# Gated attention and SwiGLU on one core: guard rows and second-layer pieces issued earlier, key loads on two queues, weight splits moved behind finished pairs

## The chip, the core and the metric

The kernel runs on one core of a Trainium2 chip. A core has a matrix engine (TensorE, PE in the profile, with its weight loads as PEld), three engines for elementwise work (VectorE or DVE, ScalarE or ACT, GpSimd or POOL) and SyncE (SP), which here only issues transfers. Each engine takes its instructions strictly in the order in which they were written and waits at each for semaphores that others raise. Transfers (DMA) between the chip's memory and the on-chip buffers are issued by an engine and then run on the core's 16 DMA engines. The metric is the device time of one execution in microseconds (us). It is the median of three runs: 1436.97 us, from 1435.83 to 1441.32.

## The reference: what is computed

```python
def _A_ref(x, wqkv, wo):                       # x: 1 x 2048 x 512
    H = 32; Dh = D // H                        # 32 heads of 16
    qkv = (x @ wqkv).reshape(B, S, 3, H, Dh)   # then split into q, k, v
    scores = jnp.einsum("bhqd,bhkd->bhqk", q, k) * Dh ** -0.5
    o = jnp.einsum("bhqk,bhkd->bhqd", softmax(scores), v)
    return o.transpose(0, 2, 1, 3).reshape(B, S, D) @ wo

def _B_ref(x, w1, w3, w2):                     # F = 1792
    return (_silu(x @ w1) * (x @ w3)) @ w2

g = _sigmoid((x * gate_w).sum(-1, keepdims=True))
return g * _A_ref(x, wqkv, wo) + (1 - g) * _B_ref(x, w1, w3, w2)
```

All of it is fp32, and no token is masked.

## The kernel before, in words

**Arithmetic.** [...] Each operand is split into a high half (a cast) and a low half (operand less high half), written hi/lo, xH/xL, wh/wl, and `three` (L94) adds high·high, high·low and low·high into one PSUM bank. So every operand passes a cast and a subtraction first, on POOL for weights and later pieces (L199, L323, L430, L500 and the line behind each), on ACT and DVE for x (L159, L160) and for the first q/k blocks (L186, L187).

**Setup (L334 to L390), written out by hand.** x comes in four blocks of 512 tokens; `transpose_x(b)` transposes block b on PE. `project_qk(0, b, wq)` makes the first 128 columns of q and of k for block b (8 heads) and stores hi and lo of both to memory (`qH_d`, `qL_d`, `kH_d`, `kL_d`), from where `load_q` and `load_k` fetch one head pair into the stacked tiles `Qt` and `Kt`. `project_v(t)` makes V for the 128 tokens of tile t; the sums of tiles 7 to 9 stay in PSUM until L389.

The softmax needs no row maximum as long as a bound on all scores is small. `squares` (ACT, then DVE) sums the squares of each head's weight columns into `rs`, `x_squares` those of each token, and `bound` (L225) multiplies the two largest and sets `flag`. `guard_rows` (L237) writes the bound into rows that go to memory (`m_d`, L247) and back into `Qt` (`load_guard`, L268). `row_maxima` (L277) reads the flag on every engine and branches at L280; the branch's body computes real maxima and is not run with these inputs. The first score (L757) stands behind the branch. `squares` reads six further weight blocks of 256 KB, which SP fetches in two groups of three (L353 and L363, issued at L123) into the three `fr` buffers. `x_gate` (DVE) sums x times gate_w for g.

**The long loop (L777).** A string of letters sets the order: Q is a score product (two matmuls, L757) with its exponential on ACT (L761), P a pair of products with V (L745) that adds up in `acc`, and F one step of `feed`, which gives both halves of PE one matmul each of other work. That other work comes in blocks of 12 or 14 matmuls from `blocks` (L652): the V tiles left, three more chunks of q/k columns, 14 chunks of the hidden layer (L406), then the second layer by token tile (L533, three parts each), then part of the output projection. A half hands its PSUM bank to the other half through a tiny DVE instruction, the tick (L718). Small PSUM banks (`f`) number three.

**Where a block's operands come from.** `load_weights(chunk)` (L312) issues a chunk's two weight fetches on SP into `fr` buffers and puts their split on POOL in the same place. `qk_done` (L424) copies a finished q/k block to a `gs` buffer (DVE, L429; two buffers), splits it on POOL (L430, L431) and stores both halves (SP, L173). `gate_done` and `up_done` form the hidden layer's values and store them to `h_d`. `load_piece(t, q)` (L509) fetches 512 (or 256) hidden rows of token tile t back from `h_d` and splits them on POOL (L500), `load_w2` does the same for the second layer's weights, whose halves take over the tiles of xH and xL. Both stand in the list `loads`, from which one entry is taken at some of the scores.

The transfers of SP and ACT share eight completion semaphores in turn, and a transfer is issued only when the one before it on its semaphore has landed.

Of the kernel before, what the change touches and what calls it, by code (L numbers as in the profile page):

```python
# [17 lines left out]
P = 128  # L18
S = 2048
D = 512  # L20
# [14 lines left out]
def gated_mix_kernel(ctx: ExitStack, tc: tile.TileContext, x, wqkv, wo, w1, w3, w2, gate_w, out):  # L35
# [31 lines left out]
    p1 = ph1.enter_context(tc.tile_pool(name="p1", bufs=1, side="right"))  # L67

# [52 lines left out]
    def load_w(c):  # L121
        w = slot("fr", F32, (P, ND, P))
        nc.sync.dma_start(w, wqkv[:, c:c + P].rearrange("(k p) n -> p k n", p=P))  # L123
        return w
# [50 lines left out]
    def project_qk(c, b, w, between=None):  # L175
        ps = psum2()
        for i in range(2):
            if i and between:
                between()
            for n, (h, xs) in enumerate(((0, xH), (0, xL), (1, xH))):  # L180
                for k in range(ND):
                    nc.tensor.matmul(ps[:, i, :], w[i][h][:, k, :], xs[b][:, k, :], start=n == k == 0,
                                     stop=n == 2 and k == ND - 1)
        hi = p1.tile([P, 2, 512], F32R, name="hi", bufs=2)
        lo = p1.tile([P, 2, 512], F32R, name="lo", bufs=2)
        nc.scalar.activation(hi, ps, AF.Copy)  # L186
        nc.vector.tensor_sub(lo, ps, hi)  # L187
        for i in range(2):
            store_qk(i, c, b, hi[:, i, :], lo[:, i, :])
# [60 lines left out]
    def load_k(j, i, b0=0, b1=NB):  # L250
        c = slice(512 * b0, 512 * b1)
        for h in range(2):
            r = 64 * h
            s = slice(DH * (2 * j + h), DH * (2 * j + h) + DH)
            for o, ks in enumerate((0, 0, 1)):
                nc.sync.dma_start(Kt[i][r + DH * o:r + DH * o + DH, c].bitcast(F32), QD[1][ks][s, c])  # L256
# [20 lines left out]
    def row_maxima():  # L277

        small = nc.values_load(flag, min_val=0, max_val=1)
        with tc.If(small < 1):  # L280
# [4 lines left out]
            for j in range(NPAIR):  # L285
# [14 lines left out]
                mxr = p1.tile([P, 2 * NT], F32, name="mxr")  # L300
# [10 lines left out]

    def load_weights(chunk):  # L312
        out = []
        for n, w in zip("13", chunk["src"]):
            r = slot("fr", F32, (P, ND, P))
            nc.sync.dma_start(r, w.rearrange("(k p) n -> p k n", p=P))
            if chunk["first"]:
                wh = slot("raw", F32R, (P, ND, P))
                wl = slot("raw" if n == "1" else "gw", F32R, (P, ND, P))
            else:  # L320
                wh = slot("fh" + n, F32R, (P, ND, P))
                wl = slot("fl" + n, F32R, (P, ND, P))
            nc.gpsimd.tensor_copy(wh, r)  # L323
            nc.gpsimd.tensor_sub(wl, r, wh)
# [17 lines left out]
    for i in range(2):  # L342
        squares(w0[i], ND * i)
    load_v()
# [8 lines left out]
    ws = [load_w(P * c) for c in range(1, ND)]  # L353
    for t in range(3):
        project_v(t)
# [3 lines left out]
    x_squares(2)  # L359
    project_qk(0, 2, wq)  # L360
    for c in range(1, ND):
        squares(ws[c - 1], c)
    ws = [load_w(D + P * c) for c in range(1, ND)]  # L363
    x_gate(2)
    project_v(4)
    x_squares(3)
    project_v(5)
    transpose_x(3)
    project_v(6)
    for c in range(1, ND):  # L370
        squares(ws[c - 1], ND + c)
    load_q(0, 0, 0)
    load_k(0, 0, 0, 3)
    project_qk(0, 3, wq, bound)
    guard_rows()
    load_guard(0, 0, 0)
    load_k(0, 0, 3, NB)
    x_gate(3)
    load_weights(chunks[0])

# [3 lines left out]
    nc.vector.tensor_scalar(omg, g, -1.0, 1.0, op0=OP.mult, op1=OP.add)  # L384

# [71 lines left out]
    def up_done(f, b):  # L457
        def done(ps):
# [6 lines left out]
            def product():  # L465
# [8 lines left out]
                if f == NF - 1 and b == 0:  # L474
                    loads[0:0] = [lambda q=q: load_piece(0, q) for q in range(2)]
# [7 lines left out]
            if f == NF - 1:  # L483
                loads.extend([lambda c=c: load_w2(c) for c in range(4 * b, min(4 * b + 4, NF))])
                if b == NB - 1:
                    loads.extend([lambda q=q: load_piece(1, q) for q in range(2)])
# [22 lines left out]
    def load_piece(t, q):  # L509
        hi, lo = (slot(SETS[t % 2][2 * q + i]) for i in range(2))  # L510
# [265 lines left out]
    pend, issued, clock = [], 0, 0  # L776
    for i, c in enumerate(order):  # L777
        clock += 1 if c != "P" else 4
        if c == "Q":
# [6 lines left out]
            while soon and order[i + 1] == "P":  # L786
                soon.pop(0)()
            if issued % 128 == (40 if issued // 128 == 5 else 12) and 1 <= issued // 128 < 8:
# [93 lines left out]
```

## Time and profile before

| | |
|---|---|
| median of the runs, and their spread | 1436.97 us (1435.83 to 1441.32) |
| the profiled execution's own time | 1436.01 us |
| its span in the trace | 1434.2 us |
| mean granted PE clock | 0.992 of full |
| PE busy | 1403.3 us |
| ACT busy | 1029.5 us |
| DVE busy | 485.7 us |
| POOL busy | 317.5 us |
| moved by DMA | 141.44 MB |

The span is the profiled execution from its first to its last instruction; 1.8 us of its own time lie around it. A row of an engine's timeline gives the start, the duration, the engine (with a q where its sequencer does it: issuing a transfer, a branch), the line, what is written from what, how many of them, and in brackets how long the engine was idle before and what ended that. A row of waits reads: engine, operation and line, what it waited for, us in total, how many times, the longest. A row of stretches gives for each engine the busy time and the number of instructions, then the granted clock of PE, the DMA engines' mean busy share and the rate. Matmuls overlap, so a matmul's duration is longer than the distance to the next one.

### The profile page before, as it was taken

The numbers are of one execution on the slowest core, as the hardware profiler recorded it, in microseconds if no ns is written. First come the engines' busy times: TensorE is split into PE (matmuls) and PEld (weight loads), VectorE is DVE, ScalarE is ACT, GpSimd is POOL, SyncE is SP. The second block draws the span as 40 slices with busy tenths as digits, with TensorE's granted clock in tenths as the row PEclk, the third lists the DMA queues.
The fourth block names the chain that finished last, engine by engine and source line by source line (L and its number), as shares of the span: only waits on it lengthen the run. The fifth ranks groups of instructions, "written<-read, shape, count | busy, mean of one in ns | idle before, by whom it ended". The sixth has DMA issues, their size and how long they took to land.

```text
span 1434.2 us, 29035 instructions
## 1 busy us (share of the span) xinstructions
PE 1403.3 (98%) x11471; PEld 835.6 (58%) x11471; DVE 485.7 (34%) x1079; ACT 1029.5 (72%) x1147; POOL 317.5 (22%) x356
## 2 busy tenths in 40 slices
PE   9879989999999999999999999989999999999998
PEld 7656555656565565655656566545655555555556
DVE  5511111154555555455555545531111110011113
ACT  4447666777777777777777777766778787788870
POOL 5011433211101110011011021552423222233240
PEclk9989999999999999999999999999999999999999
DMA  7722444543213433223232522543534443355344
GB/s 200 176 54 53 130 113 129 135 112 75 57 44 87 108 68 83 62 67 91 53 83 70 119 77 60 133 119 79 131 92 97 99 102 78 76 128 116 88 131 174
DMA packets 112863, 141.44 MB, mean 99 GB/s; under 512 B 16496, under 2 KB 70768, under 8 KB 109744
## 3 DMA queue, kind: packets, MB, share of 16 engines
q1 hardware_dynamic: 110576, 135.72, 38.4%
q10 hardware_dynamic: 2144, 3.80, 0.7%
q8 instruction: 92, 1.51, 0.5%
q14 instruction: 51, 0.42, 0.1%
HBM read 90.70 MB, written 48.76 MB: 97 GB/s over the span
## 4 chain that ended last, share of the span: by engine, by line
PE 92%; DMA 1%; POOL 1%; SPq 0%; issue 0%; ACT 0%; DVE 0%; POOLq 0%; DVEq 0%; ACTq 0%
PE acc L745 32%; PE f L406 26%; PE S L757 19%; PE f L533 11%; PE f L415 1%; PE f L619 1%; DMA fr<-in_A_wqkv_dram 0%; PE f L96 0%; PE f L97 0%; PE f L98 0%; PE S L98 0%; PE S L97 0%; PE S L96 0%; DMA sg<-h_d 0%; SPq L256 0%
## 5 line engine op out<-in xcount | busy, mean ns | idle before, releaser
L761 ACT ACTIVATE p<-S 128x1024 f32<-128x1024 f32 x1024 | 967.3, 1024 | 338.6 <-PE S L757 338.2
L745 PE MATMUL acc<-p,V 128*17 128x512 f32 x4096 | 473.7, 596 | 0.0
L757 PE MATMUL S<-Qt,Kt 50*128 50x512 f32 x2048 | 410.8, 412 | 12.5 <-SPq L280 12.2
L757 PEld LDWEIGHTS S<-Qt,Kt 50*128 50x128 f32 x2048 | 186.9, 185 | 185.1 <-issue 76.5
L745 PEld LDWEIGHTS acc<-p,V 128*17 128x17 f32 x4096 | 103.6, 97 | 278.8 <-issue 278.5
L449 DVE RECIPROCAL sg<-sg 128x64 f32<-128x64 f32 x448 | 209.6, 517 | 53.0 <-issue 50.9
L406 PE MATMUL f<-xH,fh 64*128 64x512 f32 x1024 | 205.9, 391 | 4.8 <-DVE tick L718 4.8
L406 PE MATMUL f<-xL,fh 64*128 64x512 f32 x1024 | 206.0, 392 | 0.0
L406 PE MATMUL f<-xH,fl 64*128 64x512 f32 x1024 | 205.5, 391 | 0.0
L323 POOL CAST fh<-fr 128x512 fp32r<-128x512 f32 x32 | 20.4, 637 | 443.8 <-DMA fr<-in_B_w_dram 423.4
L406 PEld LDWEIGHTS f<-xH,fh 64*128 64x128 f32 x1024 | 99.6, 187 | 26.8 <-DVE tick L718 5.2
L718 DVE MEMSET tick<- 1x1 f32 x196 | 11.6, 59 | 302.3 <-PE f L533 165.1
L406 PEld LDWEIGHTS f<-xL,fh 64*128 64x128 f32 x1024 | 100.1, 187 | 20.8
L406 PEld LDWEIGHTS f<-xH,fl 64*128 64x128 f32 x1024 | 99.1, 185 | 20.1
L533 PE MATMUL f<-xH,fh 64*128 64x512 f32 x224 | 64.9, 395 | 5.6 <-POOL fh L500 5.6
L533 PE MATMUL f<-xH,fl 64*128 64x512 f32 x224 | 66.3, 395 | 0.0
L533 PE MATMUL f<-xL,fh 64*128 64x512 f32 x224 | 65.8, 394 | 0.0
L441 DVE COPY gs<-f 128x512 f32<-128x512 f32 x56 | 38.7, 692 | 60.4 <-PE f L406 59.0
L533 PE MATMUL f<-xH,raw 64*128 64x512 f32 x192 | 56.2, 391 | 0.0
L726 DVE COPY u<-acc 128x512 f32<-128x512 f32 x32 | 22.1, 692 | 96.7 <-PE acc L745 96.7
L447 DVE TENSOR_SCALAR sg<-sg 128x512 f32<-128x512 f32 x56 | 25.3, 451 | 81.4 <-ACT sg L446 81.4
L552 DVE SCALAR_TENSOR_TENSOR y<-f,omg,y 128x512 f32<-128x512 f32 x32 | 24.0, 751 | 77.4 <-PE f L533 77.4
(224 smaller groups left out, 1350.7 us busy)
## 6 DMA issues: line engine op xcount, KB each, us to landing
Kt<-kH_d SPq DMA_DIRECT2D x124, 128.0 KB
h_d<-sg SPq DMA_DIRECT2D x56, 256.0 KB
sg<-h_d SPq DMA_DIRECT2D x43, 256.0 KB
fr<-in_B_w_dram SPq DMA_DIRECT2D x42, 256.0 KB
Qt<-qH_d SPq DMA_DIRECT2D x128, 64.0 KB
Kt<-kL_d SPq DMA_DIRECT2D x62, 128.0 KB
fr<-in_A_wqkv_dram SPq DMA_DIRECT2D x18, 256.0 KB
Qt<-qL_d SPq DMA_DIRECT2D x64, 64.0 KB
```

Of the source, the lines that this page charges most:

```text
L323: nc.gpsimd.tensor_copy(wh, r)
L406: return nc.tensor.matmul(ps, w[i == 2][r, k, :], (xL if i == 1 else xH)[b][r, k, :], start=n == 0 and not second, stop=n == 3 * ND - 1 an ...
L415: return nc.tensor.matmul(ps, (xL if i == 2 else xH)[b][r, k, o:o + P], wv[k][i == 1][r, :], start=n == 0 and not second, stop=n == 3 * ND ...
L441: nc.vector.tensor_copy(gs, ps)
L447: small.append(lambda: nc.vector.tensor_scalar(sg, sg, 1.0, None, op0=OP.add))
L449: small.append(lambda q=q: nc.vector.reciprocal(sg[:, q:q + 64], sg[:, q:q + 64]))
L533: ins = nc.tensor.matmul(ps, hs[t][q][i == 2][r, P * o:P * o + P], (w2L if i == 1 else w2H)[q][r, o, :], start=n == 0 and not second, stop ...
L552: nc.vector.scalar_tensor_tensor(y, ps, omg[:, t:t + 1], y, op0=OP.mult, op1=OP.add)
L726: nc.vector.tensor_copy(u, acc)
L745: nc.tensor.matmul(acc[r:r + DH + 1, :], V[:, k, 2 * j + h, :], p[:, h, :], start=k == 0, stop=k == NT - 1)
L757: nc.tensor.matmul(ps[:, h, :], Kt[i][r:r + 50, P * k:P * k + P], Qt[i][r:r + 50, t:t + 512], start=True, stop=True)
L761: nc.scalar.activation(p, ps, AF.Exp, scale=SCALE)
```

## The change

The edits, in the order of the program:

1. The six weight blocks for `squares` are fetched right behind the squares of the first two, issued by ACT, into six tiles of their own (pool `sqp`). The `squares` calls themselves stand between `project_v(0)`, `(1)` and `(2)`.
2. `x_squares(3)` follows `x_squares(2)`. `bound`, block 3's transpose and `guard_rows` stand ahead of `project_qk(0, 3)`; so do the first head pair's loads (all but the key loads of block 3), the loads of the guard rows, the two gate sums left, g and chunk 0's weight fetch. `project_v(6)` follows the block.
3. `project_qk` stores K before Q. The six key loads of block 3 are issued by SP for one head and by ACT for the other.
4. The split of a chunk's weights (all but the first chunk's) is put on POOL six scores after its fetch is issued.
5. The first two pieces of token tile 1 are fetched with those of tile 0, when the hidden layer's block 0 is done, into tiles (`wo2`, `wo3`) that the output weights take later. Before, they stood last in `loads`.
6. A tile in the branch that isn't run gets eight more columns.

```diff
-    def load_w(c):
-        w = slot("fr", F32, (P, ND, P))
-        nc.sync.dma_start(w, wqkv[:, c:c + P].rearrange("(k p) n -> p k n", p=P))
+    def load_w(c, tile=None, e=nc.sync):
+        w = tile if tile is not None else slot("fr", F32, (P, ND, P))
+        e.dma_start(w, wqkv[:, c:c + P].rearrange("(k p) n -> p k n", p=P))
         return w
...
-        for i in range(2):
+        for i in (1, 0):
             store_qk(i, c, b, hi[:, i, :], lo[:, i, :])
...
-    def load_k(j, i, b0=0, b1=NB):
+    def load_k(j, i, b0=0, b1=NB, e=(nc.sync, nc.sync)):
...
-                nc.sync.dma_start(Kt[i][r + DH * o:r + DH * o + DH, c].bitcast(F32), QD[1][ks][s, c])
+                e[h].dma_start(Kt[i][r + DH * o:r + DH * o + DH, c].bitcast(F32), QD[1][ks][s, c])
...
+    splits, issued = [], 0
+
+    def split(hi, lo, src):
+        nc.gpsimd.tensor_copy(hi, src)
+        nc.gpsimd.tensor_sub(lo, src, hi)
+
     def load_weights(chunk):
...
             if chunk["first"]:
...
+                split(wh, wl, r)
             else:
...
-            nc.gpsimd.tensor_copy(wh, r)
-            nc.gpsimd.tensor_sub(wl, r, wh)
+                splits.append((issued + 6, lambda a=(wh, wl, r): split(*a)))
...
     for i in range(2):
         squares(w0[i], ND * i)
+    ws = [(ND * i + c, load_w(i * D + P * c, sqp.tile([P, ND, P], F32, name=f"s{i}{c}"), nc.scalar))
+          for i in range(2) for c in range(1, ND)]
     load_v()
     project_qk(0, 0, wq, lambda: transpose_x(1))
...
     load_x(3)
-    ws = [load_w(P * c) for c in range(1, ND)]
-    for t in range(3):
-        project_v(t)
+    project_v(0)
+    for n, w in ws[:ND - 1]:
+        squares(w, n)
+    project_v(1)
+    for n, w in ws[ND - 1:]:
+        squares(w, n)
+    project_v(2)
     transpose_x(2)
     fill_k()
     project_v(3)
     x_squares(2)
+    x_squares(3)
     project_qk(0, 2, wq)
-    for c in range(1, ND):
-        squares(ws[c - 1], c)
-    ws = [load_w(D + P * c) for c in range(1, ND)]
+    project_v(4)
+    bound()
+    transpose_x(3)
+    guard_rows()
     x_gate(2)
-    project_v(4)
-    x_squares(3)
     project_v(5)
-    transpose_x(3)
-    project_v(6)
-    for c in range(1, ND):
-        squares(ws[c - 1], ND + c)
     load_q(0, 0, 0)
     load_k(0, 0, 0, 3)
-    project_qk(0, 3, wq, bound)
-    guard_rows()
     load_guard(0, 0, 0)
-    load_k(0, 0, 3, NB)
     x_gate(3)
-    load_weights(chunks[0])
-
...
+    load_weights(chunks[0])
+    project_qk(0, 3, wq)
+    load_k(0, 0, 3, NB, (nc.sync, nc.scalar))
+    project_v(6)
...
                 if f == NF - 1 and b == 0:
-                    loads[0:0] = [lambda q=q: load_piece(0, q) for q in range(2)]
+                    loads[0:0] = [lambda t=t, q=q: load_piece(t, q) for t in range(2) for q in range(2)]
...
                 if b == NB - 1:
-                    loads.extend([lambda q=q: load_piece(1, q) for q in range(2)])
                     hurry = True
...
     def load_piece(t, q):
-        hi, lo = (slot(SETS[t % 2][2 * q + i]) for i in range(2))
+        if t == 1 and q < 2:
+            both = wk.tile([P, 2, 512], F32R, name=f"wo{2 + q}")
+            hi, lo = both[:, 0, :], both[:, 1, :]
+        else:
+            hi, lo = (slot(SETS[t % 2][2 * q + i])[:] for i in range(2))
...
+            while splits and splits[0][0] <= issued:
+                splits.pop(0)[1]()
```

Where this moves instructions is shown for three engines. First ACT near the program's start; `raw<-fr` at L222 (L223 after) are the squares of the first two weight blocks, `xH1` is the high half of x block 1, `hi` that of the first q/k block. Before:

```order
L222 ACTIVATE raw_193<-fr_114 128x512
L222 ACTIVATE raw_196<-fr_116 128x512
L159 ACTIVATE xH1_236<-f_238 128x512
L159 ACTIVATE xH1_236<-f_239 128x512
L159 ACTIVATE xH1_236<-S_240 128x1024
L186 ACTIVATE hi_275<-S_223 128x1024
```

And after:

```order
L223 ACTIVATE raw_199<-fr_119 128x512
L124 DMA s01_202<-in_A_wqkv_dram 128x4x128
L124 DMA s02_204<-in_A_wqkv_dram 128x4x128
L124 DMA s03_206<-in_A_wqkv_dram 128x4x128
L124 DMA s11_208<-in_A_wqkv_dram 128x4x128
L124 DMA s12_210<-in_A_wqkv_dram 128x4x128
L124 DMA s13_212<-in_A_wqkv_dram 128x4x128
L160 ACTIVATE xH1_251<-f_253 128x512
L160 ACTIVATE xH1_251<-f_254 128x512
L160 ACTIVATE xH1_251<-S_255 128x1024
```

Six issues now stand between the squares and the copies of x block 1. The fifth (`s12`) uses the semaphore of the first V weight's fetch, the sixth (`s13`) that of the second's.

Next SP between the last q/k block's stores and the branch (L280, L281 after). Before:

```order
L173 DMA kL_d_84<-lo_655 128x512
L247 DMA m_d_85<-sg_665 32x4x512
L247 DMA m_d_85<-sg_666 32x4x512
L268 DMA Qt0_105<-m_d_85 2x1024 x2
L256 DMA Kt0_107<-kH_d_83 16x512 x2
L256 DMA Kt0_107<-kL_d_84 16x512
L256 DMA Kt0_107<-kH_d_83 16x512 x2
L256 DMA Kt0_107<-kL_d_84 16x512
L316 DMA fr_687<-in_A_wqkv_dram 128x4x128
L316 DMA fr_693<-in_A_wqkv_dram 128x4x128
L279 TENSOR_LOAD flag_129
```

And after:

```order
L269 DMA Qt0_108<-m_d_88 2x1024 x2
L323 DMA fr_641<-in_A_wqkv_dram 128x4x128
L323 DMA fr_647<-in_A_wqkv_dram 128x4x128
L174 DMA kH_d_86<-hi_678 128x512
L174 DMA kL_d_87<-lo_679 128x512
L174 DMA qH_d_84<-hi_678 128x512
L174 DMA qL_d_85<-lo_679 128x512
L257 DMA Kt0_110<-kH_d_86 16x512 x2
L257 DMA Kt0_110<-kL_d_87 16x512
L280 TENSOR_LOAD flag_132
```

The guard rows' way through memory and the weight fetches moved ahead of the last stores, and three of the six key loads went to ACT, where they stand behind `hi` of the last block and ahead of V tile 6's copy.

Last POOL, where the long loop's first weight chunk but one is split; `sg<-gs` and `gs<-gs,sg` split a finished q/k block, `fh1`, `fl1`, `fh3`, `fl3` are halves of weights. Before:

```order
L431 TENSOR_TENSOR gs_6324<-gs_6324,sg_6325 128x512
L323 CAST fh1_6334<-fr_6332 128x512
L324 TENSOR_TENSOR fl1_6335<-fr_6332,fh1_6334 128x512
L323 CAST fh3_6340<-fr_6338 128x512
L324 TENSOR_TENSOR fl3_6341<-fr_6338,fh3_6340 128x512
L430 CAST sg_6363<-gs_6362 128x512
L431 TENSOR_TENSOR gs_6362<-gs_6362,sg_6363 128x512
```

And after:

```order
L439 TENSOR_TENSOR gs_6328<-gs_6328,sg_6329 128x512
L438 CAST sg_6363<-gs_6362 128x512
L439 TENSOR_TENSOR gs_6362<-gs_6362,sg_6363 128x512
L316 CAST fh1_6338<-fr_6336 128x512
L317 TENSOR_TENSOR fl1_6339<-fr_6336,fh1_6338 128x512
L316 CAST fh3_6342<-fr_6340 128x512
L317 TENSOR_TENSOR fl3_6343<-fr_6340,fh3_6342 128x512
```

One finished pair went ahead of the split. The same happens at the next chunk's split; at the others POOL's order is as before. In the fetches of pieces, SP's two for token tile 1 moved from behind all second-layer weights to the place of tile 0's first two: three piece fetches, then the twelve loads of the next head pair and its guard rows, then the fourth.

## What the change should do to the time

> **What bounds the kernel now.** I read the busy times first, then what TensorE (PE) waits for, then stretches of two microseconds around each wait for the granted clock, then the instructions around each wait.
>
> ```profile
> PE 1403.3 (98%) x11471; PEld 835.6 (58%) x11471; DVE 485.7 (34%) x1079; ACT 1029.5 (72%) x1147; POOL 317.5 (22%) x356
> PE S L757 <- SPq L280: 12.2, 1, 12.2
> PE f L533 <- POOL fh L500: 5.6, 1, 5.6
> PE f L406 <- DVE tick L718: 4.8, 1, 4.8
> PE f L230 <- DVE am L227: 1.6, 1, 1.6
> PE f L97 <- POOL fl L200: 0.7, 1, 0.7
> ```
>
> PE is busy 98% of the span, and the change leaves all its 11,471 matmuls in place. So the time can only move through PE's waits. Three are long: A (12.2 us, before the first score), B (4.8, a q/k product), C (5.6, the first product of token tile 1). Each is a single wait. The stretches below (columns: PE, PEld, DVE, ACT, POOL busy; granted clock; DMA share; GB/s) show what else they cost.
>
> ```profile
> 72.00:74.00 2.00, 0.00 (x0) 0.00 (x0) 1.13 (x2) 0.00 (x0) 0.00 (x0) 0.87 0.18 36
> 86.00:88.00 2.00, 2.00 (x16) 1.95 (x13) 0.06 (x1) 1.32 (x2) 0.00 (x0) 0.71 1.23 229
> 198.00:200.00 2.00, 0.18 (x2) 0.18 (x4) 0.69 (x2) 0.00 (x0) 0.62 (x2) 0.95 0.79 285
> 202.00:204.00 2.00, 2.00 (x16) 0.39 (x12) 0.00 (x0) 1.02 (x1) 0.00 (x0) 0.70 0.36 132
> 960.00:962.00 2.00, 0.00 (x0) 0.00 (x0) 0.00 (x0) 0.00 (x0) 1.92 (x3) 0.74 0.75 239
> 966.00:968.00 2.00, 2.00 (x12) 0.34 (x8) 0.00 (x0) 0.95 (x1) 1.84 (x4) 0.55 0.00 0
> ```
>
> With half and full clock as the two states, a mean of 0.87 over 2 us puts the drop at 73.5, 4.5 us after PE stopped (81.17 - 12.2 = 69.0). In the same way the drop is at 199.8 in B (4.8 after the stop at 195.0) and at 961.0 in C (4.2 after 956.8). Full clock returns at 87.2, 203.2 and 967.8. From PE's restart (81.17, 199.82, 962.40) that is 6.0, 3.4 and 5.4 us at half clock, and half of it is lost: 3.0, 1.7 and 2.7 us. So A costs 15.2, B 6.5 and C 8.3 us, 30 in all.
>
> **Wait A: the order of the last q/k block.** Columns: start, duration, engine, line, instruction; SPq is SyncE issuing.
>
> ```profile
> 49.44 0.48 PE L96 MATMUL f<-fh,xH 128*128 128x512 f32 x1
> 52.32 1.11 PE L182 MATMUL S<-xH,wh 128*128 128x512 f32 x4
> 60.20 1.02 ACT L186 ACTIVATE hi<-S 128x1024 fp32r<-128x1024 f32 x1 [4.18 <-PE S L182]
> 63.39 0.44 SPq L173 DMA_DIRECT2D kL_d<-lo  x1
> 63.93 1.01 SPq L247 DMA_DIRECT2D m_d<-sg  x2
> 68.76 0.96 SPq L268 DMA_DIRECT2D Qt<-m_d  x2
> 72.99 0.42 SPq L256 DMA_DIRECT2D Kt<-kL_d  x1
> 73.45 0.97 SPq L316 DMA_DIRECT2D fr<-in_A_wqkv_dram  x2
> 81.17 1.42 PE L757 MATMUL S<-Qt,Kt 50*128 50x512 f32 x4 [12.21 <-SPq L280]
> 60.00:66.00 6.00, 6.00 (x28) 4.82 (x28) 4.49 (x11) 1.02 (x1) 0.00 (x0) 1.00 0.60 169
> ```
>
> SP stands from 64.94 to 68.76 behind the landing of the guard rows, and then issues the two guard loads, six key loads and two weight fetches before it reaches the branch. From its last issue (74.42) to PE's restart pass 6.75 us of flag load, branch and event releases. Nothing in the change touches those, so I keep 6.75.
>
> After the change the guard rows, their loads and the weight fetches stand ahead of the last block's stores, so only kH, kL, qH, qL and three key loads (the other three are ACT's) precede the branch. PE reaches the last block earlier by the 1.6 us wait for the bound and by V tile 6, now behind it: 2.9 us (49.44 to 52.32). The bound and guard rows now take two of the three small PSUM banks ahead of V tile 5; a new wait there, between 0 and 1.6 (the bound's own), is taken at 1.0, since the bound must still come through DVE. Moving the squares adds the early wait of the next part, +3.5. So the copy to hi starts at 60.2 - 1.6 - 2.9 + 1.0 + 3.5 = 60.2, where it was, and the kL store goes out at 63.4 less the places of the two q stores that no longer precede it (0.9): 62.5. Its landing is bounded by the kL store at wait B (below: 196.58 to 199.08 at latest, 2.5) and the guard rows (63.93 to 68.76: 4.8); I take 4.5, near the upper one, since the weight fetches now share the queues. Then three key loads at 0.44 (1.3), then 6.75: PE restarts at 75.1, I say 75.5 for the gate sums that ACT's copy to hi now has ahead of it. PE runs out at 69.0 - 1.6 + 1.0 + 3.5 = 71.9 and idles 3.6 us, shorter than any of the three delays (4.2, 4.5, 4.8) after which the clock fell. So A gives 81.2 - 75.5 = 5.7, and the 3.0 of half clock: 8.7.
>
> ACT's three key issues stand ahead of V tile 6's copy, and V tile 9 needs that bank: PE is waiting for the keys then anyway. Storing K before Q delays only qH and qL, whose last block the first scores don't read. The early weights of chunk 0 need no cover: their split ran on an idle POOL. The eight more columns of mxr lie in the branch that isn't taken.
>
> **The price of the moved squares.** Six weight loads move from SP (30 and 47 us) to ACT, ahead of ACT's copies of x block 1.
>
> ```profile
> 8.94 1.16 ACT L222 ACTIVATE raw<-fr 128x512 f32<-128x512 f32 x2
> 13.62 1.09 ACT L159 ACTIVATE xH<-f 128x512 fp32r<-128x512 f32 x2 [3.52 <-PE f L156]
> 16.94 1.20 PE L182 MATMUL S<-xH,wh 128*128 128x512 f32 x4 [0.22 <-DVE xL L160]
> 17.00 0.61 POOL L199 CAST fh<-fr 128x512 fp32r<-128x512 f32 x1 [2.62 <-DMA fr<-in_A_wqkv_dram]
> L123 SPq DMA_DIRECT2D fr<-in_A_wqkv_dram x8: 397/504/5077, 2.6 to 47.7; - x8
> ```
>
> ACT is free at 10.1 and needed at 13.62; six issues at the median 0.50 would take 3.0 and fit. But the transfers of SP and ACT share eight completion semaphores, and each waits for the one before it on its own. The sixth of ACT's follows the second V weight, which lands just ahead of its cast at 17.00. So ACT would issue it then and begin x block 1's copies at about 17.8 instead of 13.62: 4.2 us late, and so are the subtraction and the second block's product (21.1 instead of 16.94). The later 0.7 us wait for a V weight is absorbed: +3.5. Bounds: 0 (the weight lands in time) and 5.3 (V's fetch shares the queues with four of the six). PE is idle for 4.4 us here, a little more than the earliest drop (4.2, C), so I charge B's loss of 1.7. The +3.5 is already in the 75.5.
>
> [...]
>
> **Wait B: the split ahead of a finished pair.**
>
> ```profile
> 185.35 0.69 DVE L429 COPY gs<-f 128x512 f32<-128x512 f32 x1 [1.84 <-issue]
> 190.74 0.61 POOL L323 CAST fh<-fr 128x512 fp32r<-128x512 f32 x1 [12.30 <-DMA fr<-in_A_wqkv_dram]
> 194.59 0.62 POOL L430 CAST sg<-gs 128x512 fp32r<-128x512 f32 x1
> 196.58 0.34 SPq L173 DMA_DIRECT2D kL_d<-gs  x1
> 199.08 0.69 DVE L429 COPY gs<-f 128x512 f32<-128x512 f32 x1 [7.20 <-DMA kL_d<-gs]
> 199.82 0.80 PE L406 MATMUL f<-xH,fh 64*128 64x512 f32 x2 [4.77 <-DVE tick L718]
> ```
>
> A q/k result is copied at 186.0, but POOL stands at the split of weights that land at 190.7 and turns to the pair at 194.59. Its gs buffer comes free only when its store has landed; the DVE copy at 199.08 waited for that, the tick behind it too, and PE for the tick. With the pair ahead of the split, POOL takes it at 186.1 (two operations, 2.0), and its stores land near 191, four microseconds before the copy that PE waits behind. Next late is the following pair, still behind the split: its buffer comes free near 199, its reader wants it near 200, so I charge nothing and keep up to 1 us. B gives 4.8 + 1.7 = 6.5. The other split that moves shows no wait of PE before.
>
> **Wait C: token tile 1's first piece.**
>
> ```profile
> 897.41 1.34 POOL L501 TENSOR_TENSOR xL<-fr,xH 128x512 fp32r<-128x512 f32 x1
> 895.89 0.64 SPq L263 DMA_DIRECT2D Qt<-qH_d  x1
> 902.89 0.57 SPq L268 DMA_DIRECT2D Qt<-m_d  x2
> 957.35 1.05 SPq L499 DMA_DIRECT2D fr<-h_d  x2
> 961.74 0.61 POOL L500 CAST fh<-fr 128x512 fp32r<-128x512 f32 x1
> 962.40 0.79 PE L533 MATMUL f<-xH,fh 64*128 64x512 f32 x1 [5.63 <-POOL fh L500]
> 965.56 0.61 POOL L500 CAST fr<-sg 128x512 fp32r<-128x512 f32 x1
> ```
>
> The piece is fetched at 957.35, behind everything else, and POOL casts it at 961.74. After the change both pieces are split near 905. PE goes on at 956.8; the next piece (965.56 now) moves up by the two splits no longer ahead of it, 3.8 us, to 961.7 plus 1.9 of its own, and PE wants it about four blocks' work later, near 966. That leaves two microseconds, so I charge nothing: C gives 5.6 + 2.7 = 8.3. The price lies near 896: three of four piece fetches go ahead of SP's twelve loads of the next head pair, and the third needs a buffer that POOL frees at 898.75. The loads then end near 907 instead of 903.5. They are issued 26 scores ahead of use, 34 us at 1.32 us each ((1434.2 - 81.2)/1024), so 26 us of cover hide 4.
>
> **Sum.** Against the profiled execution's own 1436.0 (span 1434.2): -8.7 + 1.7 - 6.5 - 8.3 = -21.8, so 1414.2. The median of the runs is 1.0 above that execution: I predict 1415.
>
> **Rivals.** R1: ACT isn't held up, the sixth load finds its semaphore free. Then PE restarts at 72.0 and the 1.7 goes: 5.2 less, 1410. For it: ACT's 3.52 us of idle time ahead of 13.62 hold six issues; against it: the cast at 17.00 that waited 2.62 for its landing.
>
> R2: the last keys land late. The queues were 0.60 full in 60 to 66 and get 0.5 MB of weights ahead of the last stores, 3 us at the 169 GB/s of that row. With 3 us more twice over (store and load), PE restarts at 81 and the clock falls again: A gives nothing, 8.7 back, 1424. [...]
>
> R3, no change to be measured: the waits of B and C pass to the next pair and the next piece, whose margins are 1 and 2 us; both come back in full (14.8): 1430.
>
> R4, slower: at 896 SP is stuck behind the piece fetches, because their buffers come free only with POOL, and POOL waits for PE's last reading of the x tiles that the second-layer weights take. The loads of the next head pair come late and scores stop. It costs nothing up to 26 us, each further one in full; past 55 us (26 + 21.8 + 7) the kernel is slower by over 0.5%. Against it: POOL frees the buffer at 898.75 in the row above. A stall of 60 us would give 1449.
>
> **Chances.** Forecast (1411 to 1420) 0.58, R1 0.12, R2 0.13, R3 0.07, R4 0.10. Of R4 I leave part to mechanisms like it that I don't see. The range takes forecast, R1 and R2, 0.83, widened by the bounds of the landing (2 us down) and of the early wait: 1408 to 1427. Faster by over 0.5% (7 us, about what a measurement of this kernel can tell from no change): 0.83; R3 goes to no change, 0.07; R4 to slower, 0.10.
>
> **What would show it.** PE's wait for the branch shrinks to some 3.6 us with the clock at 1.00 after it, restart near 75.5; a new wait of about 4 us at the second block's product near 17 to 21, with ACT's copies of x block 1 behind its last weight issue; no wait of a q/k product for the tick near 195; PE's first product of tile 1 without a wait near 935, and its piece split near 890 (905 less what A and B give). I am wrong if ACT's issues don't wait, if the last keys land after 70, or if any of PE's waits outside these places exceeds 2 us.

## The result and the profile after

The median fell from 1436.40 to 1417.47 us (four runs each, the three of the table above among them; 1435.52 to 1441.32 before, 1417.2 to 1417.8 after). The ratio is 0.9861, 95% interval 0.9839 to 0.9884: the changed kernel is 18.9 us faster, 1.2 to 1.6%. The forecast was 1415, with 1408 to 1427 around it.

The profiled execution of the changed kernel has a span of 1415.7 us, 18.5 less than before (1434.2). Its busy times and the waits of PE (waited for, us in total, times, longest):

```profile
PE 1400.2 (99%) x11471; PEld 833.0 (59%) x11471; DVE 487.0 (34%) x1079; ACT 1028.9 (73%) x1147; POOL 319.5 (23%) x356
PE S L183 <- DVE xL L161: 4.5, 1, 4.5
PE f L97 <- ACT V L212: 3.1, 1, 3.1
PE f L97 <- DVE xL L161: 0.9, 1, 0.9
PE S L768 <- PEq L281: 0.6, 1, 0.6
```

The waits for the split (B, 4.8 us) and for tile 1's piece (C, 5.6) are gone, and so is the one for the bound. The 12.2 us wait ahead of the first score has become 3.1 plus 0.6. The first row is new: it is the early wait behind ACT's weight fetches.

Where the time went is best read from the same instruction in both traces, here the exponential of some of the 1024 scores (start in us, columns before, after, difference):

```
score     before    after    difference
   16      105.5    101.2     -4.33
   80      189.6    185.1     -4.43
   88      206.6    195.7    -10.96
  656      951.8    941.8    -10.00
  664      970.9    952.3    -18.63
 1016     1392.2   1373.7    -18.55
```

So the setup gives 4.4 us, wait B 6.5 and wait C 8.6. Between scores 88 and 656 the kernel after loses 1.0 again, in many small steps, while PE is busy throughout.

**Wait A after.** Rows of ACT, SP and PE around the last q/k block, the events behind the branch (how many, shortest, median and longest in ns, first and last start in us), and three stretches (columns as in the prediction):

```profile
62.32 1.01 ACT L187 ACTIVATE hi<-S 128x1024 fp32r<-128x1024 f32 x1
63.95 0.96 SPq L323 DMA_DIRECT2D fr<-in_A_wqkv_dram  x2
65.55 0.97 SPq L174 DMA_DIRECT2D kL_d<-lo  x1
72.27 0.30 SPq L257 DMA_DIRECT2D Kt<-kL_d  x1
72.68 0.60 ACT L212 ACTIVATE V<-f 128x512 f32<-128x512 f32 x1 [9.35 <-DMA kL_d<-lo]
73.33 0.79 PE L97 MATMUL f<-fh,xH 128*128 128x512 f32 x1 [3.15 <-ACT V L212]
79.44 0.93 PE L768 MATMUL S<-Qt,Kt 50*128 50x512 f32 x4 [0.62 <-PEq L281]
L281 SPq EVENT_SEMAPHORE  x8: 17/17/17, 77.6 to 78.2; - x8
L281 PEldq EVENT_SEMAPHORE  x1: 51/51/51, 78.9 to 78.9; - x1
64.00:68.00 4.00, 4.00 (x19) 3.23 (x18) 0.68 (x2) 0.00 (x0) 0.00 (x0) 1.00 1.02 178
72.00:74.00 2.00, 0.67 (x2) 0.57 (x3) 0.00 (x0) 0.60 (x1) 0.20 (x1) 0.67 0.96 104
78.00:80.00 2.00, 1.38 (x6) 0.65 (x7) 0.69 (x1) 0.00 (x0) 0.00 (x0) 0.63 0.17 45
```

SP no longer stands behind the guard rows. But the last kL store, issued at 65.55, lands only at 72.2, 6.7 us later, in a queue that is full (share 1.02). The first score comes at 79.44, 1.7 earlier than before and 3.9 later than the prediction's 75.5, of which 1.7 are the early half clock that it charged apart. PE doesn't stand idle all that time: V tile 9 runs at 73.33, late, because V tile 6's copy stands on ACT behind the key loads, and at half clock (72.7 to 79.5), so that it ends only at 78.8. So PE is the last to pass the branch (78.9; SP is through at 78.2), and the V tile holds the first score by some 0.9 us, an estimate from these two rows and from 0.25 us between SP's event and the first score where SP is the last (79.26 and 79.51 in the kernel with V tile 6 ahead of the keys). The half clock is over when the scores begin.

**The early wait, B and C after**, in rows of ACT, PE, DVE, POOL and SP:

```profile
10.26 7.14 ACTq L124 DMA_DIRECT2D s<-in_A_wqkv_dram  x4
17.45 1.09 ACT L160 ACTIVATE xH<-f 128x512 fp32r<-128x512 f32 x2 [7.87 <-DMA fr<-in_A_wqkv_dram]
20.76 1.51 PE L183 MATMUL S<-xH,wh 128*128 128x512 f32 x4 [4.55 <-DVE xL L161]
180.92 0.69 DVE L437 COPY gs<-f 128x512 f32<-128x512 f32 x1 [1.84 <-issue]
181.67 0.61 POOL L438 CAST sg<-gs 128x512 fp32r<-128x512 f32 x1 [7.65 <-DVE gs L437]
183.66 0.34 SPq L174 DMA_DIRECT2D kL_d<-gs  x1
186.26 0.61 POOL L316 CAST fh<-fr 128x512 fp32r<-128x512 f32 x1 [2.62 <-DMA fr<-in_A_wqkv_dram]
189.65 0.69 DVE L437 COPY gs<-f 128x512 f32<-128x512 f32 x1 [2.20 <-DMA kL_d<-gs]
190.43 0.06 DVE L729 MEMSET tick<- 1x1 f32 x1
883.14 4.70 SPq L506 DMA_DIRECT2D fr<-h_d  x3
892.27 0.60 POOL L507 CAST wo<-fr 128x512 fp32r<-128x512 f32 x1
893.52 0.58 SPq L269 DMA_DIRECT2D Qt<-m_d  x2
```

The four last issues of ACT take 7.14 us. The last of them starts at 17.02, right behind the landing of the second V weight, and the copies of x block 1 stand behind it. In B POOL takes the finished pair at once and splits the weights behind it. In C the piece is split at 892, and SP's loads of the next head pair end at 894.1.

### The profile page after: what moved, and what is told of

It is laid out like the page before. It is cut to its first block, busy times and chain, and to the rows that moved or that the text cites. A ratio compares the mean times of both kernels' runs of the same rounds, so it can differ in the third digit from the quotient of the medians.

```text
span 1415.7 us, 29018 instructions
## 1 busy us (share of the span) xinstructions
PE 1400.2 (99%) x11471; PEld 833.0 (59%) x11471; DVE 487.0 (34%) x1079; ACT 1028.9 (73%) x1147; POOL 319.5 (23%) x356
## 4 chain that ended last, share of the span: by engine, by line
PE 94%; ACT 0%; DVE 0%; issue 0%; ACTq 0%
PE acc L756 33%; PE f L414 27%; PE S L768 19%; PE f L544 11%; PE f L630 1%; PE f L423 1%; PE f L97 0%; PE f L98 0%; PE f L99 0%; PE S L99 0%; PE S L98 0%; PE S L97 0%; ACT p L772 0%; PE acc L99 0%; PE acc L98 0%; PE acc L97 0%
## 5 line engine op out<-in xcount | busy, mean ns | idle before, releaser
L414 PE MATMUL f<-xL,fh 64*128 64x512 f32 x1024 | 206.0, 391 | 0.0
L414 PE MATMUL f<-xH,fh 64*128 64x512 f32 x1024 | 205.9, 390 | 0.0
L414 PE MATMUL f<-xH,fl 64*128 64x512 f32 x1024 | 205.5, 390 | 0.0
L414 PEld LDWEIGHTS f<-xH,fh 64*128 64x128 f32 x1024 | 99.7, 186 | 21.8 <-DVE tick L729 0.4
L544 PE MATMUL f<-xH,fl 64*128 64x512 f32 x208 | 61.8, 390 | 0.0
L544 PE MATMUL f<-xL,fh 64*128 64x512 f32 x208 | 60.9, 391 | 0.0
L544 PE MATMUL f<-xH,fh 64*128 64x512 f32 x208 | 59.8, 391 | 0.0
L563 DVE SCALAR_TENSOR_TENSOR y<-f,omg,y 128x512 f32<-128x512 f32 x32 | 24.0, 751 | 78.2 <-PE f L544 78.2
```

What stands on the lines that cost most here:

```text
L414: return nc.tensor.matmul(ps, w[i == 2][r, k, :], (xL if i == 1 else xH)[b][r, k, :], start=n == 0 and not second, stop=n == 3 * ND - 1 an ...
L544: ins = nc.tensor.matmul(ps, hs[t][q][i == 2][r, P * o:P * o + P], (w2L if i == 1 else w2H)[q][r, o, :], start=n == 0 and not second, stop ...
L563: nc.vector.scalar_tensor_tensor(y, ps, omg[:, t:t + 1], y, op0=OP.mult, op1=OP.add)
```

## The experiments

Ratios are to the kernel before on the same chip, whose medians there were 1438.4 to 1439.4. Its runs spread over 5 us, those of the changed kernel over 1.6 in both comparisons together. To have a measure for the kernels that are set against the changed one, that was run once more beside them, with no edit:

> The changed kernel itself once more, beside the kernel before, as the measure for the experiments, whose runs of the kernel before had medians of 1438.4 to 1439.1 where the first comparison had 1436.4. Theory (the time of the changed kernel is the same in these runs, and only the kernel before scatters with where its half-clock phases fall): 1417 to 1418.5. Rival (these runs are slower by 2 us for any kernel): 1419 to 1420, and the differences of the experiments from the changed kernel shrink or grow by 2 us.

1417.86 us (1417.55 to 1418.79), ratio 0.9852 (0.9834 to 0.9870). The changed kernel's median holds to 0.4 us, so differences from 1417.5 below can be read to about half a microsecond where the runs of a kernel lie close together. Starts in a trace are less certain: the first score of this run's profiled execution is at 81.05, 1.6 later than in the first one. About half of that is there when the early wait ends (21.5 against 20.8), and about half comes from the half clock behind it, which lasted 6.8 us (19.7 to 26.5) where it had lasted 3.4.

**Each of the three parts alone.** First only the split behind the pair, on the kernel before:

```diff
-            nc.gpsimd.tensor_copy(wh, r)
-            nc.gpsimd.tensor_sub(wl, r, wh)
+                splits.append((issued + 6, lambda a=(wh, wl, r): split(*a)))
...
+            while splits and splits[0][0] <= issued:
+                splits.pop(0)[1]()
```

> The kernel before with one edit: a weight chunk's split is put on POOL six scores after its fetch. Theory (wait B is one local wait and costs its idle time and the half clock behind it): PE's 4.8 us wait for the tick goes, the clock stays at 1.00 near 200 us, the median is 6.5 us lower, 1429.9 against 1436.4. Rival (the wait passes to the next pair): a wait of 2 to 5 us at a later q/k product, gain under 3 us.

1429.35 us, ratio 0.9934 (0.9915 to 0.9954), that is 6.6 to 12.2 us lower. PE's wait for the tick is gone, and no later product takes its place. The rival is out; the forecast 6.5 lies just below the interval.

Then only the two pieces early:

```diff
-                    loads[0:0] = [lambda q=q: load_piece(0, q) for q in range(2)]
+                    loads[0:0] = [lambda t=t, q=q: load_piece(t, q) for t in range(2) for q in range(2)]
...
-                    loads.extend([lambda q=q: load_piece(1, q) for q in range(2)])
...
+        if t == 1 and q < 2:
+            both = wk.tile([P, 2, 512], F32R, name=f"wo{2 + q}")
+            hi, lo = both[:, 0, :], both[:, 1, :]
```

> The kernel before with one edit: the first two pieces of token tile 1 fetched early into tiles of their own. Theory: PE's 5.6 us wait near 957 goes with its half clock, 8.6 us lower, 1427.8. Rival (the next piece is late instead): a wait of 2 us or more at tile 1's third piece, gain 3 to 5 us.

1429.19 us, ratio 0.9935 (0.9918 to 0.9952): 6.9 to 11.8 lower, as the theory had it, and no wait at the third piece.

Then only the setup:

```diff
-                splits.append((issued + 6, lambda a=(wh, wl, r): split(*a)))
+                split(wh, wl, r)
...
-                    loads[0:0] = [lambda t=t, q=q: load_piece(t, q) for t in range(2) for q in range(2)]
+                    loads[0:0] = [lambda q=q: load_piece(0, q) for q in range(2)]
...
+                    loads.extend([lambda q=q: load_piece(1, q) for q in range(2)])
```

> The changed kernel without the other two edits (weights split at once, tile 1's pieces last in the list). Theory (the three parts add): 4.4 us lower than before, 1432.0, with the early wait of 4.5 us near 17 to 21 and PE's first score near 79.4. Rival (the parts act on each other): a difference from -4.4 of more than 2 us.

1434.77 us, ratio 0.9974 (0.9964 to 0.9984): 2.3 to 5.2 lower. The early wait (4.5) and the V tile's (3.3) are there as in the changed kernel. The three gains sum to 22.0, against 18.9 and 21.6 for the whole change in its two comparisons: the parts add, within their intervals.

**The early wait.** On the changed kernel, the fifth and sixth fetch of ACT moved behind the second block's copy:

```diff
+    ws = load_ws([(0, 1), (0, 2), (0, 3), (1, 1)])
...
     project_qk(0, 1, wq)
+    ws += load_ws([(1, 2), (1, 3)])
```

> The changed kernel with the fifth and sixth weight fetch of ACT issued behind the second q/k block's copy instead of ahead of x block 1's copies. Theory (ACT's wait for the second V weight makes the early stall, and the stall passes on to the first score through the last q/k block): the 4.5 us wait and its half clock go, the last block's hi copy starts near 57 and the first score near 74, 5.5 us lower than the changed kernel, 1412.0. Rival (the first score is set by the transfers of the last keys, whose queue is full from 64 to 72): the early wait goes but the first score comes no earlier than 77.5, at most 2 us lower, 1415.5.

1421.41 us, with runs from 1417.61 to 1424.15: 3.9 higher than the changed kernel by the medians, a miss of both. Its waits of PE, and the squares on ACT, in an execution of 1423.73 us:

```profile
PE f L97 <- ACT V L212: 10.2, 2, 7.3
PE S L183 <- DVE xL L161: 0.2, 1, 0.2
23.60 1.14 ACTq L124 DMA_DIRECT2D s<-in_A_wqkv_dram  x2
37.09 0.63 ACT L223 ACTIVATE raw<-s 128x512 f32<-128x512 f32 x1 [6.00 <-DMA s<-in_A_wqkv_dram]
40.75 0.63 ACT L223 ACTIVATE raw<-s 128x512 f32<-128x512 f32 x1 [3.03 <-DMA s<-in_A_wqkv_dram]
68.92 1.01 ACT L187 ACTIVATE hi<-S 128x1024 fp32r<-128x1024 f32 x1
84.96 1.18 PE L772 MATMUL S<-Qt,Kt 50*128 50x512 f32 x4 [2.17 <-PEq L281]
```

The early wait is gone (0.2). But the two blocks, fetched at 23.6 behind block 2 of x, land at 37 and 40.7. The copies of V stand on ACT behind their squares, and PE waits 7.3 us for a bank. The theory's second half shows all the same: the last block's copy is 6.6 later than in the changed kernel, and the first score 5.5.

So the squares of these two were moved too, behind the third q/k block's copy:

```diff
-    for n, w in ws[ND - 1:]:
-        squares(w, n)
+    squares(ws[ND - 1][1], ws[ND - 1][0])
     project_v(2)
...
     project_qk(0, 2, wq)
+    for n, w in ws[ND:]:
+        squares(w, n)
     project_v(4)
```

> As the kernel with the fifth and sixth weight fetch behind the second block's copy, but the squares of these two stand behind the third q/k block's copy, so that no copy of V waits for them. Theory (the early stall passes on to the first score): no wait over 1 us ahead of the first score but the V tile's, the last block's hi copy near 56 to 57, the first score near 73.5 to 74.5, 5 to 6 us lower than the changed kernel. Rival (the transfers are the bound: with PE's setup 6 us shorter the queue is full for all of it): the last keys land more than 8 us after their store, first score at 77 or later, at most 2.5 us lower.

1414.76 us, 2.7 lower than the changed kernel. The first score came at 77.83, 1.6 earlier, not 5 to 6. That is the rival's first score, and about its time, but for another reason: the last kL store took 6.8 us to land, no longer than in the changed kernel, while PE now waited 2.3 for the bound, whose squares came late, and 0.8 for a V weight.

Then only the sixth fetch was moved, the one that waits for the second V weight, and to a place ahead of block 2 of x:

```diff
+    ws = load_ws([(0, 1), (0, 2), (0, 3), (1, 1), (1, 2)])
     load_v()
     project_qk(0, 0, wq, lambda: transpose_x(1))
+    ws += load_ws([(1, 3)])
```

> The changed kernel with one fetch moved: the sixth weight block for the squares is issued behind the first q/k block's copy, ahead of block 2 of x in the queues; the first five stay. Theory (that one issue makes the early stall, and the first score follows the last block's hi copy at a fixed distance of about 17 us): no wait near 17 to 21, no half clock there, the last block's hi copy at 56.5 to 58, first score at 73.5 to 75, 1411.5 to 1413.5. Rival (something else holds the last block, the gate sums on DVE or the queues): hi no earlier than 60, first score no earlier than 77, 1415 or more.

1413.13 us (1412.91 to 1413.97), 4.3 lower than the changed kernel; 0.9822 of the kernel before (0.9802 to 0.9841). Its rows around the copies of x block 1, the last block and the first score:

```profile
14.35 1.09 ACT L160 ACTIVATE xH<-f 128x512 fp32r<-128x512 f32 x2 [3.53 <-PE f L157]
17.67 1.20 PE L183 MATMUL S<-xH,wh 128*128 128x512 f32 x4 [0.23 <-DVE xL L161]
59.31 1.01 ACT L187 ACTIVATE hi<-S 128x1024 fp32r<-128x1024 f32 x1
62.55 1.04 SPq L174 DMA_DIRECT2D kL_d<-lo  x1
69.29 0.30 SPq L257 DMA_DIRECT2D Kt<-kL_d  x1
75.37 0.93 PE L772 MATMUL S<-Qt,Kt 50*128 50x512 f32 x4 [0.71 <-SPq L281]
```

The copies wait for PE again, not for a landing; the early wait and its half clock are gone. The time is as forecast. The first score is 4.1 earlier: 3.0 by the last block's copy, and 1.1 behind SP's last issue, because V tile 9 is here through the branch with SP (74.8 and 75.0) and no longer behind it. That one issue made the early wait, and the wait passes on to the end. The last block's copy moved less than forecast (59.31, not 56.5 to 58), and the first score is 0.4 outside its range: PE now waits 0.8 us for a V weight, which the early wait had absorbed, and 0.5 for the bound.

**What sets the first score.** The changed kernel with V tile 6 ahead of ACT's key loads:

```diff
+    project_v(6)
     load_k(0, 0, 3, NB, (nc.sync, nc.scalar))
-    project_v(6)
```

> The changed kernel with V tile 6 written ahead of ACT's three key loads, so that its copy no longer waits for the last keys' landing; PE's and SP's order stay. Theory (SP's chain through the landing of the last keys sets the first score, and PE's last V tile only fills the time): the 3.1 us wait of the V tile goes, PE stops at 73 instead of 78.8, the first score stays within 1 us of 79.4 and runs at half clock after an idle time of 5 to 6 us, so the time is 0 to 2 us higher than the changed kernel. Rival (the V tile's detour is what ends last): the first score comes 2 us or more earlier and the time falls by 2 us.

1419.10 us, 1.6 higher. The V tile's wait is gone, the first score is at 79.51 behind SP after 5.6 us of idle time, and the clock falls at 77.2 and stays low to 84. The theory's numbers hold, but the work in the gap wasn't free: in this execution the early half clock lasted 6.8 us and the last block's copy came 0.9 later (63.24), and the first score came no later for it, since from SP's last issue it now took 5.9 us and not 6.9. So the V tile had held the first score by about 1 us. The gap without work cost more, 4.5 us at half clock behind the first score, half of it lost.

Chunk 0's weights behind the keys:

```diff
-    load_weights(chunks[0])
     project_qk(0, 3, wq)
     load_k(0, 0, 3, NB, (nc.sync, nc.scalar))
+    load_weights(chunks[0])
```

> The changed kernel with chunk 0's two weight fetches issued behind the last key loads, where they stood before the change. Theory (the full queue makes the last keys land late, 6.7 us after the issue of their store, and 0.5 MB of weights ahead of them are a good part of it): the keys land 2 to 3 us earlier, two more issues (1.0) stand ahead of the branch, the first score is 1 to 2 us earlier than 79.4. Rival (the landing has its own latency whatever stands ahead): the keys land 1 us earlier at most (the store's issue moves up by 1.0), and the first score is at 79.4 or later.

1419.16 us, 1.7 higher, though its runs (1417.70 to 1420.84) overlap those of the changed kernel; first score at 79.74. The kL store (65.31) landed at 71.1: 5.8 instead of 6.7 us, 1.2 earlier in all, and the two fetches ahead of the branch took that back. The V tile ran early, so PE idled 4.5 us ahead of the first score, with half clock from 79.4 to 82.9 behind it, which is about the 1.7. The rival was nearer: the weights explain 0.9 of the landing.

All keys on SP:

```diff
-    load_k(0, 0, 3, NB, (nc.sync, nc.scalar))
+    load_k(0, 0, 3, NB)
```

> The changed kernel with all six last key loads on SP. Theory (SP's chain sets the first score, each issue takes 0.44): three more issues, two of them ahead of the landing of the last store, so the branch is 0.5 to 1.3 us later; the V tile's copy is early, and PE idles 6 us before the first score, with half clock behind it: 1 to 3 us higher than the changed kernel. Rival (the second issuer is worth nothing, the transfers share the engines): within 0.5 us of the changed kernel.

1419.36 us, 1.9 higher, inside the theory's numbers, but not by its way: the first score is at 79.50, as with two queues, and PE idles 6.5 us ahead of it and runs at half clock from 75.3 to 85.5. SP's last issue ended 2.6 later (75.20 against 72.57), and its time from there to the score shrank from 6.9 to 4.3. That the score is no later doesn't show that the three issues are free: in the changed kernel V tile 9 was the last to release it, and SP's own events behind the branch came 1.1 later here (78.7 to 79.3 against 77.6 to 78.2).

On the kernel with the sixth fetch later, the gate sums and g behind the last block and V tile 6 ahead of the keys:

```diff
-    x_gate(2)
     project_v(5)
...
-    x_gate(3)
-    nc.scalar.activation(g, z, AF.Exp, scale=-1.0)
...
     project_qk(0, 3, wq)
+    project_v(6)
     load_k(0, 0, 3, NB, (nc.sync, nc.scalar))
-    project_v(6)
+    x_gate(2)
+    x_gate(3)
+    nc.scalar.activation(g, z, AF.Exp, scale=-1.0)
```

> As the kernel with the sixth fetch later, and the eight gate sums of x blocks 2 and 3 with g stand behind the last block, V tile 6 ahead of ACT's key loads. Theory (ACT's copy to hi waits behind g and the gate sums for 0.5 to 2 us, the V tile's detour costs under 1): first score 0.5 to 2.5 us earlier than without these two edits; PE idles 4 to 7 us before it and may run at half clock behind it, which takes 1.7 back: between 2 us lower and 1 us higher. Rival (g cost nothing): no earlier first score.

1414.48 us, 1.4 higher than without and outside the theory's numbers, first score 0.65 later (76.02). The rival: the last block's copy came no earlier (59.26 against 59.31), so g cost nothing worth having, and the idle gap (5.6) brought half clock again, from 75.7 to 79.1.

Last, on the kernel with the sixth fetch later, the first head pair's twelve loads earlier:

```diff
     project_qk(0, 2, wq)
...
+    load_q(0, 0, 0)
+    load_k(0, 0, 0, 3)
     project_v(4)
...
     project_v(5)
-    load_q(0, 0, 0)
-    load_k(0, 0, 0, 3)
```

> As the kernel with the sixth fetch later, and the twelve loads of the first head pair that need q/k blocks 0 to 2 alone are issued behind the third block, some 6 us earlier, so that they no longer stand between the guard rows and the last stores. Theory (the last keys land 6.7 us after their store because SP and the queues are full of these loads): the last kL store goes out about 1 us earlier and lands 3 to 5.8 us behind its issue, the first score is at 71.5 to 74 against 75.4, 1409.5 to 1412 against 1413.1. Rival (the landing takes 6 us or more whatever stands ahead of it): the first score no earlier than 74.3, at most 1 us lower.

1412.05 us (1411.37 to 1412.75), another 1.1 lower, between the theory's numbers and the rival's, and 0.9814 of the kernel before (0.9797 to 0.9830). It is the fastest of all. The rows of SP and the first score:

```profile
59.48 1.01 ACT L187 ACTIVATE hi<-S 128x1024 fp32r<-128x1024 f32 x1
59.87 0.96 SPq L323 DMA_DIRECT2D fr<-in_A_wqkv_dram  x2
61.77 0.34 SPq L174 DMA_DIRECT2D kL_d<-lo  x1
67.75 0.30 SPq L257 DMA_DIRECT2D Kt<-kL_d  x1
73.53 0.93 PE L772 MATMUL S<-Qt,Kt 50*128 50x512 f32 x4 [1.65 <-SPq L281]
60.00:64.00 4.00, 4.00 (x19) 3.22 (x18) 1.47 (x3) 0.49 (x1) 0.82 (x2) 1.00 0.76 231
```

The store goes out 0.8 earlier and lands after 6.0 instead of 6.7; the first score is 1.8 earlier, in the theory's range, and the clock of this execution never falls before its last 2 us. Yet the landing stays at the rival's 6 us, though the queues are fuller by 0.28 in the kernel without the edit (share 1.04 in 60 to 64). What makes up these 6 us is open.

## Why the prediction was right, and where its sizes were off

The time lies inside the range and 2.5 us above the forecast. By the prediction's own steps:

| step | forecast | measured |
|---|---|---|
| early wait of PE, and its half clock | 4.4, and 1.7 | 4.5, and 1.7 |
| first score, with those 1.7 in it | 77.2 | 79.44 |
| half clock of wait A saved | 3.0 | 2.6 |
| setup in sum | 7.0 | 4.4 |
| wait B | 6.5 | 6.5 |
| wait C | 8.3 | 8.6 |
| loss in the long loop | 0 | 1.0 |

The 2.6 are what score 16 gained beyond the first score (4.33 less 1.73). By the spans, 21.8 was forecast and 18.5 measured.

**The early wait was right to its place and size.** ACT's sixth fetch waited for the second V weight (its issue starts at 17.02), and the copies began at 17.45. The clock was at half from 21.5 to 24.9, by the same working as in the prediction:

```profile
20.00:22.00 2.00, 1.24 (x4) 1.02 (x5) 2.00 (x3) 2.00 (x7) 0.34 (x1) 0.87 0.76 262
22.00:24.00 2.00, 2.00 (x6) 1.57 (x5) 1.97 (x3) 0.79 (x4) 1.92 (x3) 0.50 0.47 173
24.00:26.00 2.00, 2.00 (x8) 1.60 (x8) 1.93 (x5) 0.00 (x0) 1.92 (x2) 0.78 1.12 305
```

That is 3.4 us, 1.7 lost, as charged. The clock fell behind the early wait in all six traces that have it (waits of 3.4 to 4.6 us). Its length was luck: 3.4 us in four of them, 6.8 in the other two, where PE worked through 5.0 of it and lost 2.5. Rival R1 is what the kernel with the sixth fetch later does: it measured 4.3 less, where R1 was worked out at 5.2.

**The mis-sized term is the landing of the last kL store.** The prediction took 4.5 us, between 2.5 and 4.8; it was 6.7, and none of the kernels with the new order had less than 5.8. By the trace's semaphore events the same store had taken 4.2 us in the kernel before (63.39 to 67.60), so the 4.5 fitted the old order. By the prediction's own signs ("if the last keys land after 70") it was wrong here: they landed at 72.2. The store also went out 1.3 later than worked out (65.55 against 62.5 + 1.7), since SP issued the loads ahead of it in one train until 64.9. Both together were partly made good by there being one key load behind the landing instead of three. This is R2 in part, though not by the fill of the queues: the 0.60 of 60 to 66 takes in time ahead of the store, and while it was on its way the share was 1.09 before and 1.14 after. What differs is what was issued ahead of it: three stores before, the first pair's loads, the weights and one store after. The weights account for 0.9 of the landing and the loads for 0.7, as the two kernels that move them show; the rest is open.

**ACT's key issues weren't free for V tile 6.** The prediction said that PE waits for the keys then anyway. It did, but the V tile then ran at half clock and released the first score some 0.9 us behind SP, so that the 6.75 us from SP's last issue to the score came out (6.9) by luck; in the other kernels of the new order, where SP was the last, it was 4.3 to 6.6. On balance the detour cost nothing: taking it away made the kernel 1.6 slower, because PE then stood idle into half clock.

**The half clock of wait A was saved for another reason than given.** The prediction had PE idle 3.6 us, shorter than the delays after which the clock had fallen, so that it would stay at full. The clock fell all the same, at 72.7, 2.5 us after PE stopped. It was back at 79.49, with the first score, after V tile 9 had kept PE busy from 73.33 to 78.8.

**Wait B had less margin than said.** The prediction had the store land four microseconds ahead of the copy that PE waits behind. It was issued at 183.66 and landed at 189.6, 5.9 later; the copy waited for it, and the tick came at 190.43. PE would have stood still from 195.0 - 4.4 = 190.6: 0.2 us. Again it is the landing that was too short, 2.5 assumed. And the 6.5 is the wait as the trace of before happened to have it: with the same wait (4.7 and 4.9 us), the half clock behind it lasted 6.8 us instead of 3.4 in the traces of the kernel with the two pieces alone and of that with the setup alone.

**Wait C** went as worked out. SP's loads near 890 end 0.7 us later than before, counted from the same score (894.1 against 903.5 - 10.1), where 4 were allowed for. Tile 1's first product came near 946, without a wait; the 935 among the prediction's signs takes the whole gain off 956.8, where its own sum for A and B gives 943. R3 and R4 did not occur.

The 1.0 us lost in the long loop was not forecast; PE shows no wait there, and its cause is open.

## What to carry to other kernels

A fetch that is moved to another engine's queue can hold up that engine's own work: look at what its semaphore waits for, issue by issue, since one of six made the whole wait of 4.5 us here. A stall on the matrix engine cost its idle time and the half clock behind it here (4.8 and 1.7 us in wait B), and filling a gap with useful work may be worth more than shortening it: with the V tile's wait gone and PE idle for 5.6 us instead, the kernel was 1.6 us slower. Before counting on a store's landing, look at what is issued ahead of it in the new order: the same store's landing took 4.2 us in the old one and 6.7 in the new.

## What the runs showed of the hardware

The clock fell after shorter idle times than the three of before suggested. In the changed kernel it fell at 72.7, 2.5 us after PE had stopped (70.2), in a wait of 3.1. In the kernel with the two pieces alone, the clock fell behind a wait of 1.9 us for the bound; behind the same wait before, 1.6 us there, it stayed at 1.00 (56 to 62 us). Rows of the kernel with the two pieces:

```profile
57.18 0.27 PE L230 MATMUL f<-rs,V 128*1 128x64 f32 x2 [1.87 <-DVE am L227]
56.00:58.00 2.00, 0.82 (x6) 0.64 (x7) 1.20 (x5) 0.32 (x1) 0.00 (x0) 0.99 0.63 157
58.00:60.00 2.00, 2.00 (x6) 1.61 (x5) 0.39 (x3) 0.00 (x0) 0.00 (x0) 0.50 0.65 92
60.00:62.00 2.00, 2.00 (x7) 1.26 (x6) 0.00 (x0) 0.00 (x0) 0.00 (x0) 0.66 0.00 0
```

The clock drops at 58.0, when PE works again, and is back at 61.4, which costs 1.7 us. So the 4.2 to 4.8 us after which it fell before were no lower bound. The table has PE's busy share in four stretches of 3.41 us, which is as long as the changed kernel's first half clock (21.47 to 24.88):

| kernel | stretch | PE busy | clock behind it |
|---|---|---|---|
| changed | 14.65 to 18.06 | 0.46 | full |
| changed | 18.06 to 21.47 | 0.21 | half |
| changed | 21.47 to 24.88 | 1.00 | full |
| two pieces alone | 54.54 to 57.95 | 0.45 | half |

PE was not idle for the whole of either stretch that half clock followed. What decides the fall is not shown by these runs, nor whether a program can choose it. In the traces of the kernel before and of the changed one, the half clocks ahead of the program's end lasted 3.41 us (199.78 to 203.20 before, 21.47 to 24.88 in the changed kernel), 6.83 us (960.96 to 967.78 before, 72.67 to 79.49 in the changed kernel) and 13.65 us (73.49 to 87.14 before).

Behind its branch SP stood for another 3.7 us before its next instruction in the changed kernel (branch at 73.9, next at 77.6), 2.6 us with all keys on SP (76.1 and 78.7) and 4.3 us with the gate sums behind the last block (70.8 and 75.1). The prediction's 6.75 us from SP's last issue to the first score is no constant: it was 6.9 in the changed kernel, where V tile 9 came last, 5.5 with the first loads earlier and 4.3 with all keys on SP.
